# A new instruction order table for a linear-attention and ELU-MLP kernel

## The chip, the cores and the metric

One NeuronCore of a Trainium2 chip. The metric is the device time of one execution in microseconds (us); each kernel was run several times, and the median is quoted. Other times in this text are us from the start of the profiled execution.

## The reference

Attention without a softmax over pairs, then a two-layer MLP on the result. In numpy, cut to what matters:

```python
# q, k, v: (8 batches, 8 heads, 576 positions, 64), float32
q_s = exp(q - max) / sum over d            # softmax along the head dimension
k_s = exp(k - max) / sum over positions    # softmax along the sequence
kv  = einsum('bhsd,bhse->bhde', k_s, v)    # 64x64 per head
a   = einsum('bhsd,bhde->bhse', q_s, kv)   # then reshaped to x: (4608, 512)
h   = x @ w_in                             # (4608, 2048)
g   = where(h > 0, h, exp(min(h, 0)) - 1)  # ELU
out = g @ w_out                            # (4608, 512)
```

## The kernel before

The program records some 813 operations (`S.add`) with their reads and writes, and then emits them in an order that five lists give, one per engine. A small model of time inside the kernel turns those lists into start times. The model decides two things of the program: how the engines' instructions are interleaved as they are emitted, and where filler matmuls go. The lists themselves were, it seems, found offline by annealing against that model (the kernel shows the model, not the search).

```python
ORDER = {
    "pe": ("30 28 32 43 45 47 50 67 54 68 70 71 69 72 82 86 93 115 103 90 129 128 137 ..."),
    "act": (...), "dve": (...), "gp": (...), "sp": (...),
}
...
    def hop(self, d, o):
        if d.eng == o.eng and not d.dma and (d.eng == "pe" or o.deps[d] == "war"):
            return 0
        return (0 if d.dma else self.OVER[d.eng] - d.early) + (160 if o.eng == "pe" else 35)

    def fill(self, seq):                     # fillers: matmuls on the identity, before the first real work
        ...
            if o.eng == "pe" and not done:
                count = int((o.start - free - 150) / (430 if free == self.SPIN_FROM else 260))
                if count > 0:
                    p = Op("pe", count * 220, self.spare(count), 0)
```

The work is cut into 16 units (one unit is two heads of each half of a batch's eight) and 9 blocks of 512 tokens. These are the pieces that the argument touches; the names in brackets are the lines in the profiles of before (in the changed kernel each is one higher).

```python
    # stage1(n): q -> exp (ACT) -> ZQ sum (DVE, L376) -> RZQ (L380) -> QS normalized (L384)
    #            k -> exp (ACT, L360); v -> VB cast, on POOL for units 2 to 5 (L372)
    # tp(n):     9 PE transposes of QS (L407), copies to qsT (ACT L414 / DVE L417)
    # kv_mm(n):  36 matmuls of 64x65 (L460); m(n): MBLK = kv / sum (DVE, L469 and two of L473)
    # ao_mm(n):  attention product (L491), copied to XT (ACT L513 / DVE L516)
    def load_w1(self, g0, g1, half, key, after=()):
        ...
            self.S.add("gp", ISSUE["gp"], lambda e, h=h: e.dma_start(...),
                       dma=f"w1{g0}{xs[0]}{h}", nbytes=..., after=after, follow=self.gpq)
            self.gpq = self.S.ops[-1]

    def kv_mm(self, n, ps, at=KV):
        ...
        return 615 if at == self.KV else 290, [f"kR{i}", ...], mm

    # hg_mm(j, g): 8 matmuls of 512 (L547), "stage-one product" into two of PSUM's eight banks
    def hg(self, j, g, ps, key, how, whole=True):
        S.add("act", ..., lambda e: e.activation(esb[:, :], P[:, :], AF.Exp), ...)            # L563
        ...
        elif how == "a":     # ACT Relu(1 - e) (L574), then one DVE pass (L576)
            S.add("act", ..., lambda e: e.activation(esb, esb, AF.Relu, bias=1.0, scale=-1.0), ...)
            S.add("dve", ..., lambda e: e.scalar_tensor_tensor(gt, P, 0.0, esb, ALU.max, ALU.subtract), ...)
        else:                # "d": DVE clamp (L580), then DVE maximum (L582)
            S.add("dve", ..., lambda e: e.tensor_scalar(esb, esb, 1.0, -1.0, ALU.min, ALU.add), ...)
            S.add("dve", ..., lambda e: e.tensor_tensor(gt, esb, P, ALU.max), ...)
    # out_mm(j, ts, jj0, jj1): GT times W2, 128 tokens by 512 columns (L592), copied and stored
```

Block 1 uses both forms: `"da"[g % 2]`, so its second stage-one product goes by way of ACT's Relu. From block 2 on all use "d".

The softmax here doesn't subtract the row's maximum and nothing guards it: scores larger than these inputs give would overflow.

## Time and profile before

| | before |
|---|---|
| median of the first 3 runs | 300.8 us (300.76 to 301.66) |
| span of the profiled execution | 299.0 us |
| PE busy | 287.1 us, 96% |
| PE waits that the profile names after 14 us | 0.5 us, ending at 14.95, and 0.4 us, ending at 54.98 |

A row of the waits view reads: who waited, for whom, us in total, how many times, the longest. In the chain of waits, a share belongs to the engine that held up the end. The prediction below shows these lines of before, and they say one thing: the matmul engine (PE) is full from 15 us to the end, and what an order can still win is the idle time at the start and about 1 us.

### The profile page before, as it was taken

To read this page: it belongs to the slowest core of one execution; us is meant where nothing else is said; L and a number is where in the kernel's file an instruction comes from. 1 tells how busy PE (TensorE), PEld (TensorE's weight loads), DVE (VectorE), ACT (ScalarE), POOL (GpSimd) and SP (SyncE) were. 2 spreads that over 40 slices of the span, in tenths; PEclk is the share of its full clock that TensorE was granted. 3 is DMA by queue.
4 is the path that set the end of the run, shared out by engine and by line. 5 is a ranking of instruction groups with operands and counts; after the bars stand their busy time and mean duration, and the time that the engine had idled before them with its cause. 6 is when DMAs were issued, how large, how long until landed. Compare 5 with 4: busy or idle time off the path is not lost.

```text
span 299.0 us, 4421 instructions
## 1 busy us (share of the span) xinstructions
PE 287.1 (96%) x1851; PEld 234.5 (78%) x1851; DVE 189.5 (63%) x244; ACT 182.3 (61%) x212; POOL 21.7 (7%) x33
## 2 busy tenths in 40 slices
PE   0899999999999999999999999999999999999995
PEld 0487877677888888888888888888888888888885
DVE  3958935985898685894568855588427256655500
ACT  5858848988977967867755766534462423432411
POOL 0860145100000000000000000000000000000000
PEclk9999999999999999999999999999999999999999
DMA  7999998994498697289546327041312302004214
GB/s 260 387 398 389 390 391 262 240 371 157 118 247 259 141 338 181 71 263 266 175 116 164 88 66 186 2 99 37 86 36 51 70 2 53 0 0 107 64 41 105
DMA packets 35443, 49.96 MB, mean 167 GB/s; under 512 B 16352, under 2 KB 16608, under 8 KB 35424
## 3 DMA queue, kind: packets, MB, share of 16 engines
q1 hardware_dynamic: 29840, 34.15, 41.3%
q0 software_dynamic: 5504, 15.47, 16.3%
q8 instruction: 14, 0.23, 0.3%
q10 hardware_dynamic: 80, 0.07, 0.1%
q14 instruction: 5, 0.04, 0.1%
HBM read 36.70 MB, written 9.44 MB: 154 GB/s over the span
## 4 chain that ended last, share of the span: by engine, by line
PE 89%; DVE 4%; DMA 3%; ACT 1%; SPq 1%; issue 0%
PE PS L592 43%; PE PS L547 41%; PE PS L491 3%; DMA QT<-QS 2%; PE PS L460 2%; DMA QR<-in_q_dram 1%; DVE ZQ L376 1%; DVE QS L384 1%; PE PS L407 1%; SPq L634 1%; DVE XT L516 0%; DVE GT L582 0%; ACT QR L356 0%; ACT qsT L435 0%; ACT ESB L563 0%; DVE MBLK L473 0%
## 5 line engine op out<-in xcount | busy, mean ns | idle before, releaser
L592 PE MATMUL PS<-W,GT 128*128 128x512 f32 (+1 forms) x592 | 141.4, 386 | 0.4 <-DVE GT L582 0.4
L547 PE MATMUL PS<-XT,W 128*128 128x512 f32 x576 | 140.5, 391 | 0.7 <-DVE RZK L469 0.5
L547 PEld LDWEIGHTS PS<-XT,W 128*128 128x128 f32 x576 | 107.1, 188 | 24.0 <-DVE XT L516 0.9
L592 PEld LDWEIGHTS PS<-W,GT 128*128 128x128 f32 x592 | 107.7, 188 | 22.1 <-DVE GT L582 0.8
L563 ACT ACTIVATE ESB<-PS 128x1024 f32<-128x1024 f32 x72 | 73.7, 1027 | 64.7 <-PE PS L547 64.3
L580 DVE TENSOR_SCALAR ESB<-ESB 128x1024 f32<-128x1024 f32 x64 | 44.4, 695 | 67.0 <-ACT ESB L563 66.4
L582 DVE TENSOR_TENSOR GT<-ESB,PS 128x1024 fp32r<-128x1024 f32 x64 | 77.7, 1217 | 1.8
L624 ACT ACTIVATE OSB<-PS 128x512 f32<-128x512 f32 x31 | 18.2, 598 | 30.9 <-PE PS L592 30.6
L376 DVE TENSOR_REDUCE ZQ<-QR 128x18 f32<-128x1152 f32 x16 | 21.5, 1344 | 7.3 <-ACT QR L356 7.2
L513 ACT ACTIVATE XT<-PS 128x512 fp32r<-128x512 f32 (+6 forms) x32 | 19.5, 608 | 7.0 <-PE PS L491 6.5
L384 DVE TENSOR_TENSOR QS<-QR,RZQ 128x1152 f16<-128x1152 f32 x16 | 21.6, 1353 | 0.3
L356 ACT ACTIVATE QR<-QR 128x1152 f32<-128x1152 f32 x16 | 18.6, 1165 | 2.9 <-DMA QR<-in_q_dram 2.9
L360 ACT ACTIVATE KR<-KR 128x1152 bf16<-128x1152 f32 x16 | 18.5, 1160 | 3.0 <-DMA KR<-in_k_dram 3.0
L435 ACT ACTIVATE qsT<-QT 128x1152 fp32r<-128x1152 f16 x12 | 14.0, 1166 | 0.7 <-DMA QT<-QS 0.7
L369 ACT ACTIVATE VB<-VR 128x1152 bf16<-128x1152 f32 (+1 forms) x12 | 13.5, 1124 | 0.7 <-DMA VR<-in_v_dram 0.7
L491 PE MATMUL PS<-qsT,MBLK 128*128 128x320 f32 (+5 forms) x64 | 13.9, 303 | 0.0
L491 PEld LDWEIGHTS PS<-qsT,MBLK 128*128 128x128 f32 x64 | 11.7, 190 | 2.6 <-DVE MBLK L473 0.2
L576 DVE SCALAR_TENSOR_TENSOR GT<-PS,ESB 128x1024 fp32r<-128x1024 f32 x8 | 9.8, 1220 | 4.2 <-ACT ESB L574 4.2
L672 PE MATMUL PS<-ID 128*128 128x512 f16 x7 | 3.3, 590 | 7.5 <-ACT QR L356 7.5
L473 DVE TENSOR_TENSOR MBLK<-PS,RZK 64x128 fp32r<-64x128 f32 x32 | 9.2, 289 | 0.9
L574 ACT ACTIVATE ESB<-ESB 128x1024 f32<-128x1024 f32 x8 | 8.5, 1060 | 0.2
L469 DVE RECIPROCAL RZK<-PS 128x2 f32<-128x2 f32 x16 | 2.6, 164 | 8.7 <-PE PS L460 7.7
(29 smaller groups left out, 59.7 us busy)
## 6 DMA issues: line engine op xcount, KB each, us to landing
out_dram<-OSB SPq DMA_DIRECT2D x62, 128.0 KB, 2.4
QR<-in_q_dram SPq DMA_DIRECT2D x12, 576.0 KB, 5.3
KR<-in_k_dram SPq DMA_DIRECT2D x12, 576.0 KB, 5.6
VR<-in_v_dram SPq DMA_DIRECT2D x12, 576.0 KB, 5.6
W<-in_moe_w_out_dram POOLq DMA_DIRECT2D x4, 1024.0 KB, 18.9
QR<-in_q_dram POOLq DMA_DIRECT2D x4, 576.0 KB, 11.4
KR<-in_k_dram POOLq DMA_DIRECT2D x4, 576.0 KB, 11.6
VR<-in_v_dram POOLq DMA_DIRECT2D x4, 576.0 KB, 8.0
```

What stands on the lines that cost most here:

```text
L356: S.add("act", t_act(1152, False), lambda e: e.activation(flat(q), flat(q), AF.Exp), key - 3, X=[f"qR{i}"], follow=self.table)
L360: S.add("act", t_act(1152, False), lambda e: e.activation(ek[:, :, :, :].rearrange("p h c d -> p (h c d)"), flat(k), AF.Exp), key - 2, X=[ ...
L376: S.add("dve", t_dve(1152), lambda e: e.tensor_reduce(self.ZQ[i][:, :, :].rearrange("p h c -> p (h c)"), q[:, :, :, :].rearrange("p h c d ...
L384: S.add("dve", t_dve(1152), lambda e: e.tensor_tensor(qso, q[:, :, :, :], rz, ALU.mult), key - 3, R=[f"qR{i}", f"RZQ{i}"], W=[f"QS{self.al ...
L491: last = e.matmul(P[:, y:y + n_], M[:, f, :], T[:, c0:c1, f * 64:f * 64 + 64], start=True, stop=True)
L513: S.add("act", t_act((h1 - h0) * n_, True), lambda e, dst=dst, src=src: e.activation(dst, src, AF.Copy), key, W=W, X=X)
L547: last = e.matmul(P[:, t * 512:(t + 1) * 512], self.W1[:, kc, tt * 128:(tt + 1) * 128], self.XT[:, kc, rc:rc + BLK], start=(kc == 0), stop ...
L563: S.add("act", t_act(1024, True), lambda e: e.activation(esb[:, :], P[:, :], AF.Exp), key, W=[f"E{i}"], X=banks)
L580: S.add("dve", t_dve(1024, 2), lambda e: e.tensor_scalar(esb[:, :], esb[:, :], 1.0, -1.0, ALU.min, ALU.add), key, X=[f"E{i}"])
L582: S.add("dve", t_dve(1024), lambda e: e.tensor_tensor(gt, esb[:, :], P[:, :], ALU.max), key, R=[f"E{i}"], W=gw, X=banks)
L592: last = e.matmul(dst, GT[:, jj, ts * 128:(ts + 1) * 128], self.W2[:, jj, c0:c1], start=(jj == 0), stop=(jj == 15))
L624: S.add("act", t_act(512, True), lambda e: e.activation(osb[:, :], src, AF.Copy), key, W=[f"O{i}0", f"O{i}1"], X=[f"b{bk}"])
```

## The change

The intent, as the edits suggest it: the model of time put the landings of W1 too early and a second key-value product (two units in one PSUM tile) too short. Both numbers were raised, the lists were annealed again, and the five new lists went in. The diff, with the lists cut to the lines of PE and GpSimd that the argument touches:

```diff
     "pe": (
-        "30 28 32 43 45 47 50 67 54 68 70 71 69 72 82 86 93 115 103 90 129 128 137 136 131 139 107 "
+        "28 30 32 45 43 47 50 67 54 68 70 71 69 72 82 86 93 115 103 90 128 129 136 137 131 107 130 "
 ... (13 lists' lines more)
     "dve": (
-        "2 4 5 0 6 7 25 26 37 27 38 39 40 41 42 36 46 49 51 52 53 56 74 75 78 80 81 85 88 89 96 100 "
+        "4 5 2 6 0 7 25 26 27 37 38 39 40 41 46 42 36 49 51 52 53 56 74 75 78 80 81 85 88 89 96 100 "
 ...
     "gp": (
-        "1 14 15 16 17 18 19 20 21 57 59 58 63 60 61 62 64 66 99 65 113 125 144 121 114 145 181 186 "
-        "189 "),
+        "1 14 15 16 17 18 19 20 21 59 57 58 63 60 61 62 64 65 66 99 125 113 144 121 145 181 186 114 "
+        "189 "),
 ... ("act" and "sp" likewise)
@@ load_w1
             self.gpq = self.S.ops[-1]
+            self.gpq.margin = 600
@@ kv_mm
-        return 615 if at == self.KV else 290, [...], mm
+        return 615 if at == self.KV else 350, [...], mm
```

In the DVE list, 25, 26, 27 are sum, reciprocal and normalization of unit 0, and 37, 38, 39 those of unit 1; 40, 41, 42 are the reciprocal and the two MBLK halves of unit 0, 36 half of the V cast of unit 1, 46 the copy of unit 1's transposes, 49 the XT copy that the first stage-one product (67 of PE) waits for.

## The prediction

> **What bounds the kernel now.** I read the page's table of busy time first, then the chain that ended last, then the waits of the matmul engine, then the timeline of the three stretches in which that engine is not full. All times are in us from the start of the profiled execution (span 299.0; the timed median is 300.8).
>
> ```profile
> PE 287.1 (96%) x1851; PEld 234.5 (78%) x1851; DVE 189.5 (63%) x244; ACT 182.3 (61%) x212; POOL 21.7 (7%) x33
> ...
> PE 89%; DVE 4%; DMA 3%; ACT 1%; SPq 1%; issue 0%
> ```
>
> PE is busy 96% of the span and carries 89% of the chain; no other engine passes 63%. An order table can't shorten PE's work, only the idle time around it. Where that lies, the engine's waits say:
>
> ```profile
> PE PS L672 <- ACT QR L356: 7.5, 1, 7.5
> PE PS L547 <- DVE RZK L469: 0.5, 1, 0.5
> PE PS L592 <- DVE GT L582: 0.4, 1, 0.4
> PE PS L407 <- DVE QS L384: 0.3, 1, 0.3
> ```
>
> The 7.5 is the start (first q load, exponential). After it only 1.2 us of waits are named in the whole run. By stretches (columns: stretch, its length, then busy us and instruction count of PE, PEld, DVE, ACT, POOL, then clock, DMA share, GB/s):
>
> ```profile
> 15.00:24.70 9.70, 9.70 (x42) 7.66 (x42) 6.23 (x8) 6.17 (x7) 5.11 (x7) 1.00 1.30 396
> 24.70:30.70 6.00, 6.00 (x30) 4.98 (x29) 4.92 (x6) 4.83 (x6) 0.00 (x0) 1.00 1.23 388
> 30.70:49.90 19.20, 19.20 (x168) 15.29 (x168) 10.80 (x18) 13.09 (x18) 7.67 (x9) 1.00 1.11 358
> 49.90:66.40 16.50, 15.94 (x136) 12.10 (x135) 15.01 (x20) 15.08 (x17) 1.88 (x2) 1.00 1.02 294
> 66.40:296.05 229.65, 229.60 (x1383) 190.68 (x1381) 143.27 (x176) 132.57 (x157) 0.00 (x0) 1.00 0.44 117
> ```
>
> From 66.4 to the end PE has 0.05 us idle in 230: nothing is to be won there. In 49.9 to 66.4 PE lacks 0.56 us and DVE and ACT are both over 90% busy: this is the only stretch of the body where order decides. Loads run at some 390 GB/s until about 46, which is what two lines of the timeline and the time to landing tell of the start:
>
> ```profile
> 12.84 0.65 POOL L336 DMA_DIRECT2D W<-in_moe_w_in_dram  x1
> ...
> DMA to landing us min/median/max: 11.9/11.9/11.9
> ```
>
> The last part of W1 is issued at 12.84 and lands 11.9 later, at 24.7, and the product that needs it starts at 24.75. The second part was issued at 9.15 and takes 5.7, so lands at 14.9, and the first product of stage one starts at 14.95. So the start is paced by loads and by vector work at once, and fits the loads within 0.1 us.
>
> **What the Trainium skill says.** "Perfetto Trace Analysis", section Optimization Strategy: find the gaps on the engine one optimizes and the semaphore that ends them. Here there is about 1 us of them behind 15. "DMA: Bandwidth & Descriptors", section Issuing engines are not separate DMA queues: loads of all issuing engines share 16 engines and interleave. The trace agrees (396, 388, 358 GB/s whoever issues), so exchanging two loads moves a landing but not the sum. "TensorE: Matmul & The Clock Gate", Part 1: the array runs at half rate until about 3.4 us of activity. The trace agrees in kind: nine transposes of L407 take 1.14 us at 10.1 and 0.52 at 36.4, though the page's clock line shows 0.9 or more throughout. "PSUM — Partial Sum Buffer", section PSUM bank collisions: guard by bank. That is why a stage-one product must wait for the DVE pass that ends the use of its two banks.
>
> **The change, part by part.** (a) The two edited numbers, 600 for W1 landings and 350 for a second key-value product, are in the kernel's own model of time. They issue no instruction; they set only which order an annealer liked, and how many filler matmuls on the identity stand in the start. (b) So the chip sees the five order lists and the fillers. I compared both built programs engine by engine; work and shapes are the same.
>
> The start. DVE now normalizes q of unit 0 before it reduces q of unit 1. Before: reduce 7.48 to 8.79, then QS0 8.71 to 10.06, QS1 10.27 to 11.63. After: QS0 from 7.5 to 8.9, reduce to 10.2, reciprocal 10.4, QS1 to 11.75. The transposes of unit 0 are 1.2 us earlier and those of unit 1 0.1 later. Fillers are 3, 3, 2, 3 instead of 5, 1, 1: four more. Cold fillers step by 0.43 us. Transposes 8.95 to 10.05, three fillers to 11.3, then the key-value product of unit 0 to 12.0 (it ended at 11.9 before). Its reciprocal then starts at about 12.05 rather than 11.95, and one of the two MBLK halves is now put behind the copy of unit 1's transposes: 12.1 to 12.5 first half, copy 0.69 once the transposes are done (13.1) to 13.85, second half to 14.1, V cast 0.75 to 14.85. Before, the V cast ended at 13.55. PE has three fillers, the attention product (about 14.2 to 14.7) and the key-value product of unit 1 after the cast, to 15.3. So the first stage-one product would start at about 15.4 and not at 14.95. If the clock is warm earlier, thanks to more fillers, much of this goes: 0 to 0.5 later, I take 0.3. It can't be much earlier than 14.9, for the second part of W1 lands then. And 40 products (40 x 0.227 = 9.1) plus the attention product (0.5) lie before the last part of W1: a start 0.3 later shows as 0.2 at 24.75.
>
> The middle, 30 to 50. On POOL the load of q for unit 2 goes before the first part of W2, and v of unit 3 before the last part. One such load is worth 1.5 us (576 KB at 390 GB/s). W2's first part comes at 28.9 (27.4 before, needed at 30.7). Its last part comes at 44.5 (43.0 before); it is needed after one more key-value product than before, at 44.3 + 0.4 = 44.7. Both hold, the second by 0.2 only. The set of PE work up to the end of the third stage-one product of block 1 is the same in both orders, so I put that end at 54.6 in both.
>
> The tight stretch. The wait of 0.39 at 54.98 (out product on the vector pass L582) goes: I reckon ACT's exponential there at 51.2 to 52.2, the DVE passes 52.5 to 54.4, ahead of PE. But the next product needs banks that come free through exponential 1.03, Relu 1.06 and DVE pass 1.22 after the second stage-one product (end 52.8): 52.8 + 3.3 + hops = 56.2, and that is the same in both. So the wait there grows from 0.25 to 0.7. After it, the new PE order puts only one pair of out products (0.45 us) where the old had two before the next stage-one product, while DVE has a reduce of 1.35 and a reciprocal of 0.27 ahead of the pass that frees those banks (59.6 + 0.1). PE is there at 56.25 + 2.15 + 0.45 + 0.71 = 59.55: 0.15 to 0.25 of waiting. The two next products wait 0.25 and 0.3 by the same count (normalization of 1.36 put before the vector pass; pass ends at 62.2 and 65.7, PE is there at 62.0 and 65.4). Each restart of PE after a wait costs 0.11 more (a first step of 0.337 instead of 0.227). At 72.5 both orders start the same product, and the new one then has one pair of out products less behind it: about +0.45. Won back: the wait at 58.3 on the k exponential (0.1), and unsure parts of the above.
>
> Sum: +0.2 (start) +0.45 (tight stretch) -0.1 = about +0.5 us.
>
> **The rivals.** First: the annealer was right, and the new order has fewer waits. For it: with later W1 landings its model is nearer to the trace, and the loads of k and v for unit 5 come earlier (v of unit 5 landed at 56.2 before). What is to be won is bounded by the waits: 0.39 + 0.25 + 0.26 (before L547 at 65.7) + some 0.4 of restarts, so 299.6 at best. Against it: the chain of exponential, Relu and vector pass does not get shorter by order. Second: a load that comes late for the now earlier need, W2's last part or k of unit 4 (now issued last of its group, landing at some 53.4 by my count, needed by ACT at 57). If W2 slips by 1 us, PE stands for 1 us at 44.7: 302.3. Third: the new order of stores and loads on SP (q of unit 6 is now issued behind nine stores and loads, at about 64.6 instead of 52.9, and needed at 72.5) holds up a later stage. It lands after about 6 us, so fits by 2 us; if not, some 1 to 2 us more. Fourth: the start is hidden anyway by the last W1 landing, so +0.3 in all.
>
> **Range and chances.** Median of these: 300.8 + 0.5 = 301.3. The floor with all waits gone is 299.6, and two of the three dangers together give 303 or so. Runs of one kernel spread from 300.76 to 301.66. Range 300.0 to 302.6. For over 2% faster 6 us of idle time would have to vanish, and there is 1.3 outside the start, which loads pace: 1%. For over 2% slower a load would have to be 5 us late: 2%. Within 2%: 97%.
>
> **What would show it.** Right: PE's busy time up by some 1 us through fillers only; first L547 between 14.9 and 15.5; the product after W1's last part at 24.7 to 25.1; a wait on a DVE pass of L576 at about 56 of 0.5 to 0.8, and two or three waits of 0.2 to 0.4 between 59 and 66; no wait from 75 on. Wrong: a wait on the W2 load near 44.7, a wait on an XT copy near 72 or later, or no PE wait at all between 54 and 66 with an end before 296.

## The result, and the profile after

| | before | after |
|---|---|---|
| median of 6 runs, same rounds | 300.9 us (300.44 to 301.66) | 300.92 us (300.74 to 301.84) |
| ratio | | 1.0006, 95% interval 0.9988 to 1.0025 |
| span of the profiled execution | 299.0 | 299.2 |

A ratio is taken over the runs of both kernels in the same rounds, so it is not quite the ratio of the medians. The change is worth nothing that the timer can see. The profile is not unchanged, though. Its busy line and the engines of its chain:

```profile
PE 287.2 (96%) x1855; PEld 234.5 (78%) x1855; DVE 189.5 (63%) x244; ACT 181.6 (61%) x212; POOL 21.9 (7%) x33
...
PE 92%; DVE 4%; ACT 2%; DMA 1%; issue 0%
```

Four more PE instructions, the fillers; the work is the same. PE's waits in the changed kernel:

```profile
PE PS L673 <- ACT QR L357: 7.6, 1, 7.6
PE PS L548 <- DVE GT L577: 0.7, 1, 0.7
PE PS L548 <- DVE XT L517: 0.2, 1, 0.2
PE PS L492 <- DVE MBLK L474: 0.2, 1, 0.2
```

The wait of 0.4 on the DVE maximum is gone, and one of 0.7 on the DVE pass behind the Relu (L577, L576 of before) has come. The start waits at other places. By the same stretches as in the prediction:

```profile
15.00:24.70 9.70, 9.46 (x60) 7.53 (x45) 6.18 (x10) 6.52 (x9) 5.57 (x8) 1.00 1.26 397
24.70:30.70 6.00, 6.00 (x29) 4.94 (x28) 5.04 (x6) 5.10 (x5) 0.00 (x0) 1.00 1.32 389
30.70:49.90 19.20, 19.20 (x170) 15.55 (x169) 11.23 (x18) 13.46 (x19) 7.79 (x9) 1.00 1.10 356
49.90:66.40 16.50, 15.80 (x137) 11.96 (x136) 14.34 (x20) 14.96 (x16) 1.22 (x1) 1.00 1.02 235
66.40:296.05 229.65, 229.65 (x1384) 191.03 (x1382) 143.55 (x176) 131.96 (x155) 0.00 (x0) 1.00 0.43 120
```

No wait on a load, and none behind 66.4, as forecast. To see more than the busy shares, I numbered PE's matmuls in program order in both traces, so that each entry of the PE list has a start. Where both orders have done the same set of work, the difference is what the change has cost up to there:

| checkpoint on PE | before | after | difference |
|---|---|---|---|
| first stage-one product starts | 14.95 | 15.39 | +0.44 |
| first out product starts | 30.70 | 31.04 | +0.34 |
| third stage-one product of block 1 starts | 52.62 | 52.91 | +0.29 |
| block 1's fourth stage-one product, a pair of out products and a pair of key-value products done | 59.61 | 59.75 | +0.14 |
| second stage-one product of block 2 and all ahead of it done | 78.11 | 78.17 | +0.06 |
| PE's last matmul ends | 296.00 | 296.06 | +0.06 |

In this pair of profiles the new order loses 0.34 in the start and wins nearly all of it back behind. The gain has to be read against more profiles, though (the experiments below give them). From the third to the fifth checkpoint, before took 25.49 and the changed kernel 25.26; but the order of before took 25.28 and 25.27 in its two other profiles (e1 and e3), and the new order 25.23 to 25.28 in five more with the Relu path and fillers. So 0.2 of the gain belongs to this one profile of before. What the new order wins for good is about 0.1, most of it between the second and the third checkpoint (21.87 against 21.93 to 21.96). The start first. The timeline of before (start, length, instruction; in brackets the idle time ahead of it and what ended it):

```profile
12.23 1.02 PE L407 MATMUL PS<-ID,QS 128*128 128x128 f16 x9
...
12.80 0.76 DVE L372 CAST VB<-VR 128x576 bf16<-128x576 f32 x1
...
13.59 0.69 DVE L417 CAST qsT<-PS 128x512 fp32r<-128x512 f16 x1
...
14.20 0.68 DVE L516 CAST XT<-PS 128x512 fp32r<-128x512 f32 x1
...
14.95 1.17 PE L547 MATMUL PS<-XT,W 128*128 128x512 f32 x4 [0.53 <-DVE RZK L469]
```

And of the changed kernel:

```profile
12.37 0.67 PE L408 MATMUL PS<-ID,QS 128*128 128x128 f16 x9
...
12.80 0.69 DVE L418 CAST qsT<-PS 128x512 fp32r<-128x512 f16 x1 [0.25 <-PE PS L408]
...
13.85 0.76 DVE L373 CAST VB<-VR 128x576 bf16<-128x576 f32 x1
...
14.64 0.69 DVE L517 CAST XT<-PS 128x512 fp32r<-128x512 f32 x1
...
15.39 1.21 PE L548 MATMUL PS<-XT,W 128*128 128x512 f32 x4 [0.24 <-DVE XT L517]
```

From 12 us on DVE is a queue without slack here. Before, it casts V first and copies the transposes some 0.3 after they are done; after, it stands 0.25 for PE's transposes, and all behind it, the XT copy included, is late. In the tight stretch PE waited twice before:

```profile
54.98 1.19 PE L592 MATMUL PS<-W,GT 128*128 128x512 f32 x4 [0.39 <-DVE GT L582]
...
56.26 2.14 PE L547 MATMUL PS<-XT,W 128*128 128x512 f32 x8
```

The second of these waits, 0.25 by the starts of the matmuls, is under what the view names. In the changed kernel there is one:

```profile
54.18 1.06 ACT L575 ACTIVATE ESB<-ESB 128x1024 f32<-128x1024 f32 x1
...
55.27 1.23 DVE L577 SCALAR_TENSOR_TENSOR GT<-PS,ESB 128x1024 fp32r<-128x1024 f32 x1 [0.95 <-ACT ESB L575]
...
56.55 2.11 PE L548 MATMUL PS<-XT,W 128*128 128x512 f32 x8 [0.65 <-DVE GT L577]
```

Relu, vector pass, product: the chain that the prediction named, with PE standing for it (0.65 by the view, 0.81 by the starts of the matmuls). And one wait of before that the prediction didn't count, on the same kind of pass in front of an out product at 74.35:

```profile
73.07 1.22 DVE L576 SCALAR_TENSOR_TENSOR GT<-PS,ESB 128x1024 fp32r<-128x1024 f32 x1 [2.23 <-ACT ESB L574]
74.35 0.76 PEld L592 LDWEIGHTS PS<-W,GT 128*128 128x128 f32 x4 [0.42 <-DVE GT L576]
74.35 1.19 PE L592 MATMUL PS<-W,GT 128*128 128x512 f32 x4
```

PE's step into that product was 0.387 and the next 0.335 where 0.227 is the rule, so 0.27 lost. The changed order has another out product ready at this place (its matmuls run on at 74.09), and loses nothing.

### The profile page after: what moved, and what is told of

Its sections match the earlier page's. It is cut to its first block, busy times and chain, and to the rows that moved or that the text cites. A ratio compares the mean times of both kernels' runs of the same rounds, so it can differ in the third digit from the quotient of the medians.

```text
span 299.2 us, 4429 instructions
## 1 busy us (share of the span) xinstructions
PE 287.2 (96%) x1855; PEld 234.5 (78%) x1855; DVE 189.5 (63%) x244; ACT 181.6 (61%) x212; POOL 21.9 (7%) x33
## 4 chain that ended last, share of the span: by engine, by line
PE 92%; DVE 4%; ACT 2%; DMA 1%; issue 0%
PE PS L593 43%; PE PS L548 43%; PE PS L492 3%; PE PS L461 2%; DMA QR<-in_q_dram 1%; DVE GT L577 1%; PE PS L408 1%; ACT ESB L575 1%; ACT ESB L564 1%; PE PS L673 1%; DVE MBLK L474 0%; DVE QS L385 0%; DVE ZQ L377 0%; DVE GT L583 0%; ACT QR L357 0%
## 5 line engine op out<-in xcount | busy, mean ns | idle before, releaser
L577 DVE SCALAR_TENSOR_TENSOR GT<-PS,ESB 128x1024 fp32r<-128x1024 f32 x8 | 9.8, 1224 | 5.1 <-ACT ESB L575 5.0
L673 PE MATMUL PS<-ID 128*128 128x512 f16 x11 | 4.4, 517 | 7.6 <-ACT QR L357 7.6
L461 PEld LDWEIGHTS PS<-VB,KR 64*64 64x64 bf16 x576 | 5.5, 107 | 3.0 <-issue 1.1
```

## The experiments

Eleven kernels, one of them the best of all. In every one the outputs were correct. "Rest" is the time from the first out product to PE's last matmul, and "start" is the time from the first DVE reduce to the first stage-one product. The first reduce begins when the first q load has landed, and that varied from 5.79 to 6.06 among profiles, so the difference is taken from it. "Clock" is when the trace's clock record has the array at full rate (the clock line of the page reads 9 throughout and does not show it).

| profiled run | start | clock | first out product | rest | PE ends | median | ratio to before, 95% |
|---|---|---|---|---|---|---|---|
| before | 9.04 | 12.96 | 30.70 | 265.31 | 296.00 | 300.9 | |
| after | 9.33 | 11.45 | 31.04 | 265.02 | 296.06 | 300.92 | 1.0006 (0.9988 to 1.0025) |
| e1_numbers | 9.12 | 13.23 | 30.58 | 265.13 | 295.71 | 301.13 | 1.0004 (0.9987 to 1.0021) |
| e2_old_start | 9.04 | 13.15 | 30.62 | 264.99 | 295.61 | 300.54 | 0.9984 (0.9971 to 0.9996) |
| e3_new_start | 9.66 | 12.24 | 31.18 | 265.13 | 296.31 | 301.17 | 1.0001 (0.9987 to 1.0014) |
| e4_reduce_first | 9.72 | 13.78 | 31.42 | 265.03 | 296.44 | 301.04 | 0.9994 (0.9982 to 1.0006) |
| e5_two_step | 10.02 | 12.96 | 31.59 | 265.61 | 297.20 | 300.79 | 0.9993 (0.9977 to 1.0009) |
| e6_copy_behind_cast | 9.28 | 13.31 | 30.70 | 265.05 | 295.75 | 300.59 | 0.9981 (0.9966 to 0.9996) |
| e7_xt_first | 9.17 | 13.76 | 30.93 | 264.98 | 295.91 | 300.84 | 0.9988 (0.9974 to 1.0001) |
| e8_no_fillers | 9.78 | 19.63 | 33.02 | 265.28 | 298.30 | 303.06 | 1.0061 (1.0046 to 1.0076) |
| e9_two_step_cast_later | 9.68 | 12.24 | 31.19 | 264.66 | 295.85 | 300.79 | 0.9986 (0.997 to 1.0002) |
| e10_old_start_cast_later | 9.29 | 13.54 | 30.70 | 264.98 | 295.68 | 300.73 | 0.9989 (0.9973 to 1.0005) |
| e11_all_three | 9.09 | 11.46 | 30.58 | 264.68 | 295.26 | 300.14 | 0.9965 (0.995 to 0.998) |

The before runs of the three groups (e1 to e4, e5 to e8, e9 to e11) had medians of 301.2, 301.19 and 301.22. Times decide little here; the columns taken from the traces decide, and they are of one profile each.

### e1_numbers: the two numbers alone

```diff
 (order table of before)
+            self.gpq.margin = 600
-        return 615 if at == self.KV else 290, ...
+        return 615 if at == self.KV else 350, ...
```

> The order table of before with the two new model numbers (600 and 350) alone. Built, its instructions and fillers are those of before; only two waits name their semaphores in another order. Both theories: ratio 1.000 within 0.002, first stage-one product at 14.9 to 15.1 us, the wait before the product at 56.26 as before (0.25). It serves as the control for noise: what its span differs from before's 299.0 by is noise, and I expect up to 0.3 us.

Measured: 1.0004, as good as nothing, and the program is the one of before. Its profile: span 298.7 against 299.0, PE's end 295.71 against 296.00. In the profile of before the last part of W1 landed at 24.71 and PE stood 0.11 for it; in this one it landed at 23.94 and PE stood for nothing. The 0.3 between these two is the noise against which any single profile has to be read, and the old order's rest is 265.13 to 265.31. Most of the difference in the rest is a wait of 0.26 at 65.68 in before, which e1 does not have. The two numbers by themselves are thus of no effect on the chip; they can act only through the lists.

### e2_old_start and e3_new_start: the start exchanged

```diff
 e2: changed kernel, with before's first 8 PE, 12 ACT and 22 DVE entries
 e3: kernel before, with the changed kernel's
```

> The changed kernel with the start of before (first 8 entries of PE, 12 of ACT, 22 of DVE). Theory A (the parts add: the late start costs 0.34 us at the first out product, and the rest of the new order is about 0.3 better than the old): first stage-one product at 14.95 to 15.1, first out product at 30.7 instead of 31.04, and the end 0.3 us before the changed kernel's, span some 298.8. Theory B (the vector chain of the tight stretch at 51 to 66 resets the clock, the start is swallowed there): the first out product is earlier, but the product that waits at 56.55 in the changed kernel starts at 56.5 again, and the span stays at 299.1 to 299.2. Ratio to before 0.999 by A, 1.0005 by B, both within 2%.

> The kernel before with the new start (the same entries). Theory A: first stage-one product at 15.25 to 15.4, first out product at 31.0, everything behind it 0.3 later than in before, span 299.3. Theory B: the waits of 0.46 and 0.25 at 55 to 56 shrink by 0.3 and the span stays at 299.0.

Measured: theory A in both. With the old start the changed kernel's first out product comes at 30.62 and PE ends at 295.61, 0.45 ahead of the changed kernel; with the new start the old order's first out product comes at 31.18 and PE ends at 296.31, 0.60 behind its control run e1. The rest is 264.99 and 265.13, what it was with the other start. So in the traces the parts add, and the tight stretch swallows nothing. The timer is less clear. e3's 1.0001 (0.9987 to 1.0014) cannot tell 0.3 us from nothing, and the profile of e1 is the fastest of its six runs, which flatters the 0.60; against the profile of before itself it is 0.31. The old start with the new rest is the first version to beat the kernel before, at 0.9984, by an amount just clear of the interval; among eleven versions that could be chance. It was not timed in the same rounds as the changed kernel.

That run had also lost something on the way. It waits at 54.9 for the DVE maximum as before did, and the reason is a clamp of 1.64 where 0.69 is usual; it comes up again in e5.

### e4_reduce_first: which part of the new start is slow

```diff
-  dve: ... 25 26 27 37 38 39 ...
+  dve: ... 25 26 37 27 38 39 ...
```

> The changed kernel with one exchange on DVE: the reduce of unit 1 before the normalization of unit 0, as in before (the fillers follow the model: 5, 0, 1, 3). If the late start comes from dependent DVE neighbours (two more pairs in which an instruction waits for its predecessor's result, each losing about 0.12 us of overlap): normalization of unit 1 ends 5.7 us after the first reduce starts, not 6.0, and the first stage-one product starts 0.25 to 0.3 earlier relative to the landing of the first q load. Rival: the fillers and the place of the copy of unit 1's transposes between the two MBLK halves delay it; then the normalization ends earlier but the product starts as late as in the changed kernel (15.2 to 15.4).

Measured: the normalization of unit 1 ended 5.69 after the first reduce began, and 6.01 in the changed kernel, so the two dependent neighbours do cost 0.3. It was of no use: the first product started at 9.72, later than in the changed kernel. The rival is right. What took its place (timeline of this run):

```profile
12.35 1.17 PE L408 MATMUL PS<-ID,QS 128*128 128x128 f16 x9
...
13.02 0.69 DVE L418 CAST qsT<-PS 128x512 fp32r<-128x512 f16 x1 [0.46 <-PE PS L408]
```

In this run the array came to full rate at 13.78, so the nine transposes took 1.17 and not 0.67, and DVE stood 0.46 for them. This points to the copy.

### e6_copy_behind_cast: the copy put back

```diff
-  dve: ... 40 41 46 42 36 49 ...
+  dve: ... 40 41 42 36 46 49 ...
```

> The changed kernel with one DVE instruction moved: the copy of unit 1's transposes goes behind the second MBLK half and the V cast, as in before (the three fillers ahead of the attention product fall away with it). Theory C (the copy, put ahead of them, makes DVE wait for PE's transposes, 0.25 us when the array clock opens at 11.5, 0.4 to 0.5 when it opens at 13.8, and everything behind it on DVE is late by that): no such wait, XT ends 0.25 to 0.5 earlier relative to the first reduce, the first stage-one product 9.0 to 9.1 us after the first reduce starts (9.33 in the changed kernel, 9.66 and 9.72 in the two runs with a late clock, 9.04 and 9.12 in before). Rival (fillers and normalization order): 9.3 or more.

Measured: DVE no longer stands for the transposes, although the clock was late again (13.31); the first product starts at 9.28, with the normalization still in the slow order:

```profile
11.27 0.71 PE L461 MATMUL PS<-VB,KR 64*64 64x65 bf16 x36
...
12.04 0.17 DVE L470 RECIPROCAL RZK<-PS 128x2 f32<-128x2 f32 x1 [0.22 <-PE PS L461]
...
13.68 0.69 DVE L418 CAST qsT<-PS 128x512 fp32r<-128x512 f16 x1
```

The runs whose copy stands ahead of the cast have 9.33, 9.66, 9.68, 9.72 and 10.02; all others with fillers have 9.04 to 9.29. I had expected 9.0 to 9.1, so 0.2 was too much hoped for. The dependent neighbours do not explain it: the normalization had ended at 11.82, and DVE then stood 0.22 at the reciprocal (12.04) for PE's first key-value product, which came 5.46 after the first reduce (5.28 in before), behind three fillers. Nor is 9.28 outside of what the whole old start gives: e10 has 9.29 (there the V cast stood 0.22 for a load). The ratio of 0.9981 is as good as that of the whole old start. The edit took away three fillers as well, those ahead of the attention product. They were not what held it: in the changed kernel they were over at 13.69, the second MBLK half at 13.82, and the attention product began at 13.87; e3, e5 and e9 have the same order (in e4 the fillers held it by some 0.1). So most of the start's loss is this one move, and its size goes with when the array clock opens: 0.3 where it opened early (11.45), 0.6 to 1.0 in the four profiles where it opened at 12.24 to 13.78. The changed kernel's own profile had the earliest opening of all its kind (11.45), which flatters it.

### e7_xt_first: can the start be better than in both

```diff
 (on top of e2)
-  dve: ... 42 36 46 49 51 ...      pe: ... 67 54 68 70 71 69 72 ...
+  dve: ... 42 36 49 46 51 ...      pe: ... 67 68 54 69 70 71 72 ...
```

> A try to beat both: the changed kernel with the old start and, on DVE, the copy of unit 1's transposes behind the XT copy, and on PE the attention product of unit 1 behind two stage-one halves, so that nothing of unit 1 stands before the first product. First product at 14.3 to 14.9 (bounded by the landing of the second part of W1, 14.3 to 15.0 in the runs so far) instead of 15.0; the product that needs the last part of W1 at 24.3 to 24.7 instead of 24.8, where that part's landing (23.9 to 24.7 in the runs so far) takes over as the bound. If the start is worth something: span 0.1 to 0.4 under that of the old-start run (298.7), ratio to before 0.997 to 0.998. If loads bound it: a wait on W1 at 24 and the same end.

Measured: a miss. The first product started at 15.18 and not at 14.3 to 14.9. The second part of W1 had landed at 14.57, so loads did not hold it, and no wait on W1 at 24 either (landed 24.12, needed at 25.01). The clock opened at 13.76, the attention product took 0.95 where 0.7 is usual, and a gap of 0.25 between the end of the XT copy (14.92) and the product I can't explain. So whether the start can be won on is left open; this was not the way.

### e8_no_fillers: do the eleven fillers pay

```diff
-                if count > 0:
+                if False:
```

> The changed kernel without its eleven filler matmuls. If fillers pay: the array clock opens only after some us of real work, at 16 us or later, so transposes and first products take double (0.107 per transpose, 0.43 per 512-wide product) and the first out product is 1 to 2 us later, ratio 1.003 to 1.007. If they only stand in the way (rival: they delay the first key-value product to 11.5): first product 0.1 to 0.3 earlier and the end the same or earlier.

Measured: 303.06, 0.6% slower. The clock opened at 19.63, and the first products ran at half rate:

```profile
12.00 1.14 PE L408 MATMUL PS<-ID,QS 128*128 128x128 f16 x9 [0.54 <-DVE QS L385]
...
15.73 2.08 PE L548 MATMUL PS<-XT,W 128*128 128x512 f32 x4
```

The first stretch of four matmuls of 512 columns takes 2.08 here and 1.21 with fillers. The fillers are worth 2 us, more than any order tried here. That they stand in the way (the first key-value product waits behind three of them) counts for little beside that.

### e5_two_step: is the Relu chain what PE waits for

```diff
-  self.hg(1, g, ..., key, "da"[g % 2], g > 1)
+  self.hg(1, g, ..., key, "d" if g == 1 else "da"[g % 2], g > 1)
   (231 moves from the ACT list to the DVE list, ahead of 232)
```

> The changed kernel with the second stage-one product of block 1 on the path exponential, DVE clamp (0.69), DVE maximum (1.22) instead of exponential, ACT Relu (1.06), DVE (1.22). Theory A (the three-step chain behind that product sets when the third-next product may write its banks): the wait of 0.8 at 55.5 to 56.55 shrinks by about 0.3 to 0.4, since 1.06 becomes 0.69; the product after it starts at 56.2. DVE gets 0.69 more to do, so of this at most 0.3 reaches the end: span 0.0 to 0.3 under the changed kernel's 299.2, ratio 0.999 to 1.000. Rival (DVE as a whole is the bound in 51 to 66): the wait moves to the next two products and the end is the same or 0.3 later.

Measured: unclear at first. The profiled run took 302.1, another 301.92, and four 300.61 to 300.83. In the profile the product that waits started 4.27 after the end of block 1's second stage-one product, whose banks it takes over, and not 3.63. The lines that tell why:

```profile
52.51 1.51 POOL L373 CAST VB<-VR 128x1152 bf16<-128x1152 f32 x1 [2.97 <-DMA VR<-in_v_dram]
52.93 1.64 DVE L581 TENSOR_SCALAR ESB<-ESB 128x1024 f32<-128x1024 f32 x1
```

A clamp of 0.69 took 1.64 because GpSimd was at its cast. The Trainium skill has this: "SBUF — State Buffer", section Who interferes with whom, says that GpSimd and a DVE `tensor_scalar` in its two-port mode share a pair of ports under an exclusive lock. The traces agree that they exclude each other: in the five profiles in which they met with the cast ahead, both were through 1.85 to 2.06 after the cast began, and 1.15 + 0.69 = 1.84 is what they take one after the other. In before this cast stands at 56.26, between two clamps; the new table loads v of unit 5 ahead of k of unit 4, the cast comes at 51.7 to 53.2, and it falls on the clamp in e2, e4, e5 and e7 (and in e8, where all is 2 us later). In the profile of the changed kernel it began at 52.84, half a microsecond after the clamp had begun (52.37 to 53.06), which kept its 0.69. So the new order has a danger that neither I nor the kernel's model had seen. It costs time here only together with the two-step path: the stretch from the third to the fifth checkpoint took 25.87 in e5, but 25.23 to 25.28 in e2, e4 and e7, as without the collision. That e5's other slow run (301.92) collided too is likely, but it has no profile.

### e9_two_step_cast_later and e10_old_start_cast_later: the collision taken away

```diff
-  gp: ... 145 181 186 114 189
+  gp: ... 145 181 114 186 189
 (e9: on e5. e10: on e2)
```

> The two-step path of the earlier run once more, and on GpSimd the load of k for unit 4 issued before that of v for unit 5, so that GpSimd's cast of that v begins at some 54.5 to 55 us and not at 52.5. Theory D (that run's profile shows no effect of the shorter chain because its clamp of 0.69 began while the cast ran and took 1.64; the same collision makes its slow runs of 302): no clamp over 1.0 us between 50 and 60, the waiting product starts 3.2 to 3.35 us after the end of the second stage-one product (3.63 in the changed kernel, 4.27 in the collided run), and no run above 301.5. Rival (the shorter chain is worth nothing, DVE is the bound): 3.6 again. Span 298.7 to 299.2 with the start as it is.

> The old-start run with the same exchange of the two GpSimd loads. Its clamp took 1.64 at 51.96 and its PE waited 0.51 and 0.19 one after the other. Theory D': without the collision the first of these goes and the second grows to 0.81, since the product that waits last is tied to the second stage-one product alone (3.63 us behind it): the end does not change, span 298.6 to 298.8. Rival: the collision cost 0.5 and the span falls to 298.2.

Measured in e9: theory D. The cast begins at 54.74, both clamps take 0.69, the product starts 3.32 behind the second stage-one product, and no run is above 301.1.

```profile
54.39 0.69 DVE L581 TENSOR_SCALAR ESB<-ESB 128x1024 f32<-128x1024 f32 x1
54.74 1.35 POOL L373 CAST VB<-VR 128x1152 bf16<-128x1152 f32 x1 [5.96 <-DMA VR<-in_v_dram]
...
56.38 2.12 PE L548 MATMUL PS<-XT,W 128*128 128x512 f32 x8 [0.38 <-DVE GT L583]
```

PE's wait is 0.38 instead of 0.65, and the rest falls from 265.02 to 264.66: the whole gain of the shorter chain arrives at the end. Measured in e10: theory D'. Two waits become one, the product stands 3.64 behind the second stage-one product, and the rest is 264.98 as with the collision. That distance is 3.63 or 3.64 in all ten profiles with the Relu path, those of the old order included, whatever the clamps did. Without the two-step path a delayed clamp only moves the wait from one product to the one before it, since the later one is tied to the Relu chain.

### e11_all_three: the parts together

```diff
 changed kernel + old start (e2) + cast later (e9, e10) + two-step path (e5)
```

> The candidate for best: the changed kernel with the old start, the cast later and the two-step path. If the parts add: 298.7 less 0.3, span 298.3 to 298.5, median 300.1 to 300.3, ratio to before 0.997 to 0.998. If the tight stretch gives the 0.3 back at the next products: 298.7.

Measured: 300.14 (five runs, 300.12 to 300.25), ratio 0.9965, interval 0.995 to 0.998. Within 2% of before, but faster clear of the noise. The changed kernel was not timed in the same rounds; its interval against before (0.9988 to 1.0025) lies apart from this one. The five runs lie closer together than those of any other version. At the start the second part of W1 landed at 14.88 and the XT copy ended at 14.83; the product began at 14.94, and in this trace the two cannot be told apart. The rest is 264.68, and the stretch between the third and the fifth checkpoint took 24.93, as in e9 (24.91).

## Why the prediction was right, and where not

The time (300.92) lies within the range of 300.0 to 302.6, and "within 2%" was the outcome. The reason for the narrow range was right: PE full from 15 us on, about 1 us of waits behind it. The sum of +0.5 was not what the pair of profiles showed, +0.06; but against e1, which is the program of before, the changed kernel's PE ends 0.35 later, and the timer's interval (-0.4 to +0.75 us) holds all three. That the two medians agree so closely is in part luck. PE's busy time rose by 0.1 and not by the 1 forecast: the fillers took 1.05 more (4.36 against 3.31), but with the early clock the second nine transposes took 0.67 and not 1.02 and the first key-value product 0.48 and not 0.71. By the prediction's own steps:

1. *The two numbers issue no instruction.* Right; e1 shows it.
2. *The start, first product at about 15.4, of which I took +0.3, and +0.2 behind W1's last part.* The working was right and the discount wrong: the first product came at 15.39, and it shows as +0.47 at the product behind W1's last part (25.23, forecast 24.7 to 25.1) and as +0.34 at the first out product. Part of that 0.44 is a q load that landed 0.15 later; against that, the clock opened early in that one profile, and in e3 the same start cost 0.60. The cause was named (the copy between the MBLK halves), beside two that mattered less; e4 and e6 tell them apart. "If the clock is warm earlier, much of this goes" was right.
3. *The middle, both W2 loads hold.* Right: the last part of W2 landed at 44.20, no wait. The first pair of out products in need of it began at 44.96.
4. *The wait at 54.98 goes, that before the next product grows from 0.25 to 0.7.* Right: 0.65 to 0.7 in the views. The 0.25 was counted by the starts of the matmuls, and by that measure it is 0.81.
5. *Then three waits of 0.15 to 0.3, +0.45 in all.* This is the step that failed, as a size: nothing was lost here. PE reached the first two of these later than reckoned, for the wait of step 4 and the late start had already been paid, and so waited 0 and 0.08; the third was 0.22 as in before (0.26). And a wait of before with its restart, 0.27 at 74, was not in the account at all, because I had read PE's named waits, where it does not appear: the weight load's row has it. The new rest is 264.98 to 265.05 in its six profiles with the Relu path and with fillers, 0.1 faster than the old one in e1 and e3 (265.13), not 0.35 slower; the 0.3 against the profile of before holds a wait of that one profile.
6. *Rivals.* The first (the annealer was right) holds for the body alone, and by 0.1 only. The loads of the second and third didn't come late. The fourth (the start is hidden by W1) fails: e2 and e3 show the start passing to the end in full.

Where did the gain go that the annealer expected? By the kernel's own model there was none to lose. I evaluated it for both tables under both sets of numbers (start of the last store; this is the model, no measurement):

| | old numbers | new numbers |
|---|---|---|
| old table | 294.09 | 294.78 |
| new table | 294.55 | 294.85 |

Even under the new numbers the new table scores 0.07 worse than the old one. The chip says +0.06, or +0.35 against e1. The new numbers are not plainly nearer to the traces either. With 600 the last landing of W1 is put at 24.5, without at 23.9; thirteen profiles show 23.5 to 24.7, most 24.1 to 24.2. The pair of key-value products, 0.905 in the old model and 0.965 in the new, takes PE 0.71 and some 0.1 of restart.

What stays open: the spread of a microsecond among runs of one kernel (before: 300.4 to 301.9) has no single cause shown here. W1's landing, the clock's opening and the collision are three that differ from profile to profile, and e11, which has one of them less, spread least; but e9 and e10, without the collision too, spread over 0.67 and 0.97 us.

## What to carry to other kernels

When one engine is full, judge a new order by checkpoints on that engine at which both orders have done the same work; that splits a null result into a loss and a gain, and the better halves can be joined (here 0.16% in e2, and 0.35% in e11 with the two-step path added). Profile the unchanged kernel more than once: two thirds of the gain that the first pair of profiles showed was a wait that only one of them had. Don't put an instruction on a queue without slack behind work whose duration depends on the array clock, and keep GpSimd's casts off DVE clamps that a full engine waits for (0.69 became 1.64). Before annealing under a changed model, score the old table under it: if the new one isn't better by its own model, there is nothing to run.

## What the Trainium skill lacked or had wrong

- "SBUF — State Buffer", section Who interferes with whom: it says that whoever issues first holds the ports and only the other blocks. In five profiles (e2, e4, e5, e7, e8) both were lengthened. The GpSimd cast began first and ended 1.09 after the clamp's start whatever its lead (0.21 to 0.42), so it took 1.30 to 1.51 where 1.15 is usual; the clamp took 1.64 in each, not 0.69. Where the clamp began first (the changed kernel and e9), it kept its 0.69 and only the cast grew, to 1.22 and 1.35, as the page has it.
- "TensorE: Matmul & The Clock Gate", Part 1: it puts the opening at some 3.4 to 4 us of activity, give or take 0.5. Here, with fillers from 7.3 to 7.6 us on and no gap on PE over 0.35, it came 3.9 to 6.2 us later, from 11.45 to 13.78, in twelve profiles; without them at 19.63, 10.6 us after the first transposes. The same Part says that the activity window of 3413 ns runs free of the kernel's start; the first full window then ends one to two windows, 3.4 to 6.8 us, after the first filler (an estimate from that figure), which holds all twelve. The clock records fit the window too: full rate lasts 286.72 us in twelve profiles and 283.31 in e8, 3.41 less. So it is the 0.5 that is too narrow here, not the mechanism.
- "VectorE: DVE Perf Modes", section The DRAIN you can't avoid: no figure for a dependent neighbour; its one comparison, eight copies with a semaphore after each and with one after the last only, found equal times. Two more dependent pairs among six DVE instructions cost 0.3 (6.01 against 5.69); independent neighbours began 0.08 to 0.09 before the end of the one ahead, dependent ones 0.03 behind it.
- On no page that I read: PE's restart after a wait, a first step of 0.33 to 0.34 where 0.227 is the rule, so 0.11 more than the wait itself. The second matmul's weights there start to load 0.107 behind the start of the first matmul (54.98). The same step stands behind key-value products without any wait (102.98 and 126.83 in before).
